# Two merged loads of a linear-attention and SwiGLU kernel as four loads of 128 pieces

## The chip, the core and the metric

The kernel runs on one core of one Trainium2 chip. TensorE (PE in the profile) multiplies matrices, with weight loads in a row of their own (PEld); VectorE (DVE), ScalarE (ACT) and GpSimd (POOL) do the elementwise work; SyncE (SP) issues most transfers. The metric is the device time of one launch in microseconds.

## The reference, cut to what matters

The input x is 2048 rows of 512 bf16 values. The output is x plus a linear-attention block plus a gated feed-forward block, both of the layer-normalised rows xn.

```python
xn = _layernorm(x, axis=-1)
return x + _A_ref(xn, A_wqkv, A_wo) + _B_ref(xn, B_w_gate, B_w_up, B_w_down)
# A: q, k, v = xn @ wqkv in 32 heads of 16;  phi(t) = where(t > 0, t + 1, exp(t)) + 1e-6
#    kv = phi(k)^T v;  z = sum of phi(k);  o = (phi(q) kv) / (phi(q) z + 1e-6);  o @ wo
# B: (silu(xn @ w_gate) * (xn @ w_up)) @ w_down
```

## The kernel before

The 2048 rows are cut into 16 tiles of 128 rows, one row per partition. For each tile the program takes mean and variance (bn_stats, line 300, and bn_aggr, line 303), forms xn, transposes it, projects it to K and Q with 4 matmuls each (contraction of 512 in 4 blocks of 128), turns K and Q into their positive features, and adds the outer product of xn and the K features into four PSUM banks (gtacc, line 668). After the 16 tiles come 56 steps of the feed-forward block (line 870), between which the attention is divided by its denominator (lines 1015 to 1057) and output tiles are made and stored (lines 1059 to 1094).

The program is a list of instructions written out by hand, one list per engine, each run in order. A helper (line 43) adds the waits that reads and writes of named buffers need; every transfer has a semaphore of its own. So the place of a call in the source is its place in its engine's queue, and an engine that waits holds up all that stands behind it.

Tiles 0 to 3 go another way than the rest. K and Q are projected from the centred tile, and the division by the standard deviation is put into ScalarE's reading of the projection. Tiles 0 and 1 are centred on TensorE: traw (line 440) transposes the raw tile with an identity, and tcorr (line 452) adds minus the mean with a matmul of ones by a diagonal. For tile 0 that diagonal (line 401) comes from a sum of the row's two halves on VectorE (line 391), for tile 1 from ScalarE (line 308). Tile 2 is centred on VectorE (line 381) and transposed on TensorE (line 488). Tile 3 is centred on VectorE (line 470) and transposed by a transfer (line 479).

The order of the projections of tiles 0 to 3 is by hand as well (lines 720 to 817). Q's third block (c = 2) is used for tile 0, then for tile 1; then the fourth (c = 3) for tile 0, its PSUM bank is read by ScalarE (line 618), and the fourth for tile 1 (lines 752 to 756). Each such matmul (line 543) waits for its own block's name, and one load that brings two blocks sets both names at once. Then follow both projections of tile 2 and K features of tile 0 on GpSimd (line 625); gtacc of tile 0; tile 3 (line 530); gtacc of tiles 1 and 2. VectorE's list in the same part is: statistics of tiles 1, 2; centring of 2; statistics of 3; line 583 for tile 0; centring of 3; statistics of 4, 5, 6; then xn (line 317) and the K features (line 632) of the first tiles.

The loads stand ahead of all that (lines 253 to 263), on SyncE's queue, in the order x 0, K's blocks 0 and 1, K's block 2, x 2, Q's block 0, Q's block 1, x 3, Q's blocks 2 and 3, x 4 and 5, x 6 and 7; x 1 and K's block 3 go by ScalarE's queue. The remaining x tiles go in pairs behind tile 3's transpose (lines 737, 738, 773, 810).

How rows lie in tiles is set by NLONE (line 200). A tile below NLONE holds 128 successive rows, so that each partition gets one piece of 1 KB per tile. The rows from NLONE on are dealt out so that a partition holds successive rows in successive tiles: a load of two such tiles is 128 pieces of 2 KB. The same function (line 202) maps the output's rows, so input and output agree. A weight block is 128 rows of 1 KB; a load of two blocks is 256 pieces.

Of the kernel before, what the change touches and what calls it, by code (L numbers as in the profile page):

```python
# [109 lines left out]
def bass_parallel_sum__linear_attn_block__swiglu_ffn__prompt_kernel(  # L110
# [13 lines left out]
    pe, act, dve, pool, sp = nc.tensor, nc.scalar, nc.vector, nc.gpsimd, nc.sync  # L124
    bf, f32 = dt.bfloat16, dt.float32

    with contextlib.ExitStack() as es:
# [69 lines left out]

        NLONE = 4  # L200

        def rows(v, t0, n):
            if t0 < NLONE:
                return v[t0 * P:(t0 + n) * P, :].rearrange("(t p) d -> p t d", p=P)
            return v[NLONE * P:, :].rearrange("(p t) d -> p t d", t=NT - NLONE)[:, t0 - NLONE:t0 - NLONE + n, :]

        def xload(eng, h, t0, n, after=()):
            K.dma(
                eng, lambda: h.dma_start(x_sb[:, t0:t0 + n, :], rows(xin, t0, n)),  # L209
                r=list(after), w=[("x", t0 + i) for i in range(n)],  # L210
            )

        def wqkv_load(eng, h, name, i, c0, n, after=()):
            K.dma(
                eng,
                lambda: h.dma_start(  # L216
                    wqkv_sb[:, c0:c0 + n, i * D:(i + 1) * D],
                    A_wqkv[c0 * P:(c0 + n) * P, i * D:(i + 1) * D].rearrange("(c p) f -> p c f", p=P),
                ),
                r=list(after), w=[(name, c) for c in range(c0, c0 + n)],  # L220
            )
# [36 lines left out]
        wqkv_load("sp", sp, "wq", 0, 0, 1)  # L258
        wqkv_load("sp", sp, "wq", 0, 1, 1)
        xload("sp", sp, 3, 1)  # L260
        wqkv_load("sp", sp, "wq", 0, 2, 2)
        xload("sp", sp, 4, 2)
        xload("sp", sp, 6, 2)

        cw = nc.const_aps.tensor(1.0, (P, P), bf)
# [907 lines left out]
```

## Time and profile before

| what | value |
|---|---|
| median of 3 runs | 210.54 us (210.31 to 211.08) |
| profiled execution | 210.56 us |
| its span | 209.3 us |
| TensorE busy | 205.0 us (98%) |
| VectorE, ScalarE, GpSimd busy | 119.7, 71.8, 72.2 us |
| TensorE's granted clock | 1.00 |
| read from HBM | 9.70 MB |

The span runs from the first to the last recorded instruction or transfer; the device time holds a little more around it. A line of the timeline gives start and duration in us, engine, line of the source, operation, what is written from what, shapes, and a count; in square brackets stands how long the engine had been idle before and what ended that. [...] A row of a transfer group gives the size in KB and the time from its issue to its landing.

### The profile page before, as it was taken

The numbers are of one execution on the slowest core, as the hardware profiler recorded it, in microseconds if no ns is written. First come the engines' busy times: TensorE is split into PE (matmuls) and PEld (weight loads), VectorE is DVE, ScalarE is ACT, GpSimd is POOL, SyncE is SP. The second block draws the span as 40 slices with busy tenths as digits, with TensorE's granted clock in tenths as the row PEclk, the third lists the DMA queues.
The fourth block names the chain that finished last, engine by engine and source line by source line (L and its number), as shares of the span: only waits on it lengthen the run. The fifth ranks groups of instructions, "written<-read, shape, count | busy, mean of one in ns | idle before, by whom it ended". The sixth has DMA issues, their size and how long they took to land.

```text
span 209.3 us, 2809 instructions
## 1 busy us (share of the span) xinstructions
PE 205.0 (98%) x998; PEld 94.5 (45%) x1017; DVE 119.7 (57%) x245; ACT 71.8 (34%) x127; POOL 72.2 (34%) x91
## 2 busy tenths in 40 slices
PE   8999999999999999999999999999999999999996
PEld 4444444444444444444444444444444444444444
DVE  4799988336365874637355746365556545374122
ACT  6877666966643331312112312213031213121000
POOL 2537987668032543223041422240424132221200
PEclk9999999999999999999999999999999999999999
DMA  6765645894696011010201110102011010110201
GB/s 197 219 184 79 127 100 102 258 364 153 206 356 49 11 39 25 28 25 25 52 0 50 28 28 22 50 0 53 5 45 25 25 28 28 49 27 27 53 25 50
DMA packets 30127, 16.84 MB, mean 80 GB/s; under 512 B 20896, under 2 KB 29344, under 8 KB 30112
## 3 DMA queue, kind: packets, MB, share of 16 engines
q1 hardware_dynamic: 29824, 16.39, 30.0%
q10 hardware_dynamic: 288, 0.26, 0.4%
q8 instruction: 8, 0.13, 0.2%
q14 instruction: 7, 0.06, 0.1%
HBM read 9.70 MB, written 2.10 MB: 56 GB/s over the span
## 4 chain that ended last, share of the span: by engine, by line
PE 91%; DVE 3%; DMA 2%; SPq 1%; issue 1%; POOL 1%; DVEq 0%
PE psum L870 44%; PE psum L1075 23%; PE psum L516 9%; PE psum L1064 7%; PE psum L668 6%; DMA wqkv_sb<-in_A_wqkv_dram 2%; PE psum L530 2%; SPq L216 1%; DVE pkq L592 1%; SPq L209 1%; POOL prod L1019 1%; PE psum L543 0%; DVE xn_sb L317 0%; DVE den L1027 0%; DVE pkq L891 0%
## 5 line engine op out<-in xcount | busy, mean ns | idle before, releaser
L885 ACT ACTIVATE sg<-psum 128x512 bf16<-128x512 f32 x56 | 33.4, 599 | 106.0 <-PE psum L870 103.6
L870 PE MATMUL psum<-xnT,wg_sb 128*128 128x512 bf16 x222 | 57.2, 379 | 0.2 <-issue 0.2
L870 PE MATMUL psum<-xnT,wu_sb 128*128 128x512 bf16 x216 | 55.8, 379 | 0.4
L1019 POOL TENSOR_TENSOR prod<-pkq,zb 128x512 f32<-128x512 bf16 x16 | 18.6, 1163 | 55.9 <-DVE pkq L592 55.9
L870 PEld LDWEIGHTS psum<-xnT,wu_sb 128*128 128x128 bf16 x224 | 21.9, 98 | 26.4
L870 PEld LDWEIGHTS psum<-xnT,wg_sb 128*128 128x128 bf16 x224 | 21.7, 98 | 26.2 <-issue 0.2
L1088 DVE TENSOR_TENSOR out_sb<-psum,x_sb 128x512 bf16<-128x512 f32 (+2 forms) x17 | 11.2, 661 | 36.2 <-PE psum L1075 36.2
L1043 POOL TENSOR_TENSOR pqn<-pkq,rden 128x512 bf16<-128x512 bf16 x16 | 16.9, 1058 | 36.6 <-DVE rden L1037 36.6
L891 DVE TENSOR_TENSOR pkq<-psum,sg 128x512 bf16<-128x512 f32 x28 | 19.2, 686 | 17.1 <-PE psum L870 14.6
L891 DVE TENSOR_TENSOR xn_sb<-psum,sg 128x512 bf16<-128x512 f32 x28 | 18.8, 672 | 13.8 <-PE psum L870 13.3
L1075 PE MATMUL psum<-wd_sb,xn_sb 128*128 128x512 bf16 (+2 forms) x126 | 25.7, 355 | 0.0
L1075 PE MATMUL psum<-wd_sb,pkq 128*128 128x512 bf16 x108 | 25.1, 379 | 0.2
L516 PE MATMUL psum<-wqkv_sb,xnT 128*128 128x512 bf16 x95 | 22.5, 379 | 0.1
L660 POOL TENSOR_TENSOR zacc<-zacc,pkq 128x512 f32<-128x512 f32 x15 | 17.4, 1157 | 5.0 <-DVE ek L583 4.6
L1075 PEld LDWEIGHTS psum<-wd_sb,xn_sb 128*128 128x128 bf16 x126 | 11.8, 98 | 12.5
L1075 PEld LDWEIGHTS psum<-wd_sb,pkq 128*128 128x128 bf16 x112 | 11.0, 98 | 13.2
L1064 PE MATMUL psum<-m_sb,eq 128*128 128x512 bf16 (+2 forms) x67 | 16.4, 366 | 0.1
L668 PE MATMUL psum<-pkq,xn_sb 128*128 128x512 bf16 x61 | 15.6, 379 | 0.2
L516 PEld LDWEIGHTS psum<-wqkv_sb,xnT 128*128 128x128 bf16 x96 | 9.4, 98 | 11.3
L1027 DVE TENSOR_REDUCE den<-prod 128x32 f32<-128x512 f32 x16 | 10.9, 684 | 5.9 <-POOL prod L1019 5.9
L300 DVE BATCH_NORM_STATS2 stats<-x_sb 128x6 f32<-128x512 bf16 x16 | 10.9, 680 | 1.1 <-DMA x_sb<-in_A_x_dram 1.1
L592 DVE SCALAR_TENSOR_TENSOR pkq<-pkq,eq 128x512 bf16<-128x512 bf16 x16 | 11.1, 692 | 0.6
(78 smaller groups left out, 139.7 us busy)
## 6 DMA issues: line engine op xcount, KB each, us to landing
out_dram<-out_sb SPq DMA_DIRECT2D x15, 128.0 KB, 1.7
wg_sb<-in_B_w_gate_dram SPq DMA_DIRECT2D x2, 896.0 KB, 7.5
wu_sb<-in_B_w_up_dram SPq DMA_DIRECT2D x2, 896.0 KB, 5.9
wd_sb<-in_B_w_down_dram SPq DMA_DIRECT2D x1, 1792.0 KB, 11.1
x_sb<-in_A_x_dram SPq DMA_DIRECT2D x6, 256.0 KB, 3.2
wqkv_sb<-in_A_wqkv_dram SPq DMA_DIRECT2D x2, 256.0 KB, 3.6
wqkv_sb<-in_A_wqkv_dram SPq DMA_DIRECT2D x1, 512.0 KB, 7.7
wo_sb<-in_A_wo_dram SPq DMA_DIRECT2D x1, 512.0 KB, 8.7
```

Of the source, the lines that this page charges most:

```text
L516: (lambda c=c: pe.matmul(banks[b], xnT[:, c, t * P:(t + 1) * P], wqkv_sb[:, c, lo:lo + D], start=(c == 0), stop=(c == NDC - 1),))
L592: lambda: dve.scalar_tensor_tensor(out=dst, in0=src, scalar=0.0, in1=e, op0=ALU.max, op1=ALU.add,),
L660: lambda: pool.tensor_tensor(out=zacc[:, :], in0=zacc[:, :], in1=pk, op=ALU.add),
L668: (lambda c=c: pe.matmul(banks[4 + c], xn_sb[:, t, c * P:(c + 1) * P], pkq[:, t, 0, :], start=(t == 0), stop=(t == NT - 1),))
L870: (lambda c=c: pe.matmul(banks[b], w_sb[:, c, fc * P:(fc + 1) * P], xnT[:, c, C * 512:(C + 1) * 512], start=(c == 0), stop=(c == NDC - 1),))
L885: lambda: act.activation(sg[:, j % NSG, :], banks[gb], ACT.Silu),
L891: lambda: dve.tensor_tensor(out=hT(C, fc), in0=banks[ub], in1=sg[:, j % NSG, :], op=ALU.mult,),
L1019: lambda: pool.tensor_tensor(out=p, in0=pkq[:, t, 1, :], in1=zb[:, :], op=ALU.mult),
L1043: lambda: pool.tensor_tensor(out=pqn[:, t % NPN, :].rearrange("p (i g h e) -> p g i h e", i=NB, g=NG, e=DH), in0=pkq[:, t, 1, :].rearrange ...
L1064: (lambda g=g: pe.matmul(dst, pqnT(t)[:, g, :], m_sb[:, g, lo:hi], start=(g == 0), stop=False,))
L1075: (lambda fc=fc: pe.matmul(dst, hT(C, fc)[:, jj * P:(jj + 1) * P], wd_sb[:, fc, lo:hi], start=False, stop=(fc == NFC - 1),))
L1088: lambda: dve.tensor_tensor(out=o, in0=src, in1=x_sb[:, t, lo:hi], op=ALU.add),
```

## The change

The boundary NLONE goes from 4 to 6, so tiles 4 and 5 hold 128 successive rows each, and the ten tiles behind them are dealt out over partitions in tens rather than twelves, in input and output alike. The merged load of Q's blocks 2 and 3 becomes two loads, and the merged load of x 4 and 5 becomes two loads, in the same place of SyncE's queue. Tile 0's mean from two half sums, named with the change, is in the kernel before already (lines 388 to 406) and not in the diff.

```diff
-        NLONE = 4
+        NLONE = 6
 
         def rows(v, t0, n):
             if t0 < NLONE:
@@
         xload("sp", sp, 3, 1)
-        wqkv_load("sp", sp, "wq", 0, 2, 2)
-        xload("sp", sp, 4, 2)
+        wqkv_load("sp", sp, "wq", 0, 2, 1)
+        wqkv_load("sp", sp, "wq", 0, 3, 1)
+        xload("sp", sp, 4, 1)
+        xload("sp", sp, 5, 1)
         xload("sp", sp, 6, 2)
```

## The prediction

> **What bounds the kernel now.** I read the page first, then the busy time of each engine by stretch, then the chain of waits and the merged timeline of the first 20 us.
>
> ```profile
> span 209.3 us, 2809 instructions
> PE 205.0 (98%) x998; PEld 94.5 (45%) x1017; DVE 119.7 (57%) x245; ACT 71.8 (34%) x127; POOL 72.2 (34%) x91
> ```
> ```profile
> 0.00:8.36 8.36, 7.03 (x35) 3.29 (x36) 4.47 (x15) 6.12 (x14) 2.89 (x13) 1.00 0.78 233
> 8.36:20.00 11.64, 11.59 (x53) 5.30 (x55) 10.92 (x31) 8.47 (x16) 6.05 (x10) 1.00 0.50 132
> 20.00:47.20 27.20, 27.04 (x124) 12.35 (x126) 18.77 (x42) 19.49 (x36) 20.63 (x30) 1.00 0.72 187
> 47.20:207.50 160.30, 159.39 (x788) 73.56 (x801) 85.31 (x158) 37.72 (x63) 42.64 (x40) 1.00 0.20 51
> ```
>
> In the second fence the first two numbers are the stretch and its length, the third PE's busy time. TensorE is idle 1.33 us before 8.36 and nearly never after it (0.05, 0.16 and 0.91 us in the other stretches, at a granted clock of 1.00). So TensorE sets the end, and a gain can only come from the idle time ahead of 8.36; it reaches the end if nothing behind 8.36 is late for the earlier TensorE. The span is 209.3 us, the profiled execution took 210.56 us, so 1.26 us lie around the span; the median of the runs is 210.54, so a sum against the profiled execution stands for the median too.
>
> The last wait on a transfer is the one that the change touches:
>
> ```profile
> 4.12 4.19 DMA wqkv_sb<-in_A_wqkv_dram
> 8.36 1.04 PE psum L543 x4
> ```
> ```profile
> 3.65 0.43 SPq L209 DMA_DIRECT2D x_sb<-in_A_x_dram  x1
> 4.12 0.44 SPq L216 DMA_DIRECT2D wqkv_sb<-in_A_wqkv_dram  x1
> 4.61 0.94 SPq L209 DMA_DIRECT2D x_sb<-in_A_x_dram  x2
> 8.36 1.04 PE L543 MATMUL psum<-wqkv_sb,xcT 128*128 128x512 bf16 x4 [0.50 <-DMA wqkv_sb<-in_A_wqkv_dram]
> 9.15 0.69 DVE L300 BATCH_NORM_STATS2 stats<-x_sb 128x6 f32<-128x512 bf16 x1 [0.38 <-DMA x_sb<-in_A_x_dram]
> ```
>
> The merged load of Q's blocks 2 and 3 is issued at 4.12 and lands at 8.31; TensorE sat idle 0.50 us for it. The merged load of x 4, 5 is issued behind it, and VectorE sat idle 0.38 us until bn_stats of tile 4 at 9.15. These two waits are all that the change can take away.
>
> **The change, part by part.** SyncE issues one load per 0.47 us whatever its size (3.65 to 4.12). Now: wq block 2 at 4.12, block 3 at 4.59, x 4 at 5.06, x 5 at 5.53, x 6, 7 at 6.00 instead of 5.08. Two issues are added, 0.94 us of SyncE's queue. The next instruction there is a transpose that waits for VectorE until 8.79:
>
> ```profile
> 8.79 1.29 SPq L479 DMA_TRANSPOSE xcT<-xc_sb  x1
> 10.13 1.04 SPq L209 DMA_DIRECT2D x_sb<-in_A_x_dram  x2
> ```
>
> SyncE is free at about 6.5, 2.3 us ahead of it: no cost. Without this cover it would be the 0.94 us itself. No instruction of another engine is added or moved. Tile 0's half sums (line 391) and their diagonal (line 401) stand in the code of before and not in the diff, so this half of the title costs and brings nothing.
>
> When do the four loads land? Issue to landing of the single loads, then of the merged ones (median in the last column), in order of issue: wq 0, wq 1, x 3; then wq 2 with 3, x 4 with 5, x 6 with 7.
>
> ```profile
> wqkv_sb<-in_A_wqkv_dram SPq DMA_DIRECT2D x1, 128.0 KB, 3.7
> wqkv_sb<-in_A_wqkv_dram SPq DMA_DIRECT2D x1, 128.0 KB, 3.6
> x_sb<-in_A_x_dram SPq DMA_DIRECT2D x1, 128.0 KB, 3.5
> ...
> wqkv_sb<-in_A_wqkv_dram SPq DMA_DIRECT2D x1, 256.0 KB, 4.2
> ...
> x_sb<-in_A_x_dram SPq DMA_DIRECT2D x1, 256.0 KB, 4.5
> ...
> x_sb<-in_A_x_dram SPq DMA_DIRECT2D x1, 256.0 KB, 4.7
> ```
>
> A 128 KB load per 0.47 us keeps the delay level (3.7, 3.6, 3.5), so the backlog does not grow; 256 KB per issue makes it grow. The price of a single load at this place has no row. Lower bound 3.5 us from its issue, as x 3 just ahead; upper bound the merged loads' 4.2 to 4.7. I take 3.5, the nearest row of the same size: wq 2 at 7.6, wq 3 at 8.1, x 4 at 8.6, x 5 at 9.0, x 6, 7 at 9.5 to 10.7 (3.5 to 4.7 from 6.00).
>
> [...]
>
> Pieces: the page of the transfers shows the merged x loads as 2 KB pieces, the rest as 1 KB.
>
> ```profile
> DMA packets 448, 0.67 MB, mean 223 GB/s; under 512 B 49, under 2 KB 193, under 8 KB 448
> ```
>
> That is the window 6.5 to 9.5: 255 packets lie between 2 and 8 KB, which are the 128 pieces each of x 4, 5 and x 6, 7 but one. After it x 4, 5 are 256 pieces of 1 KB; the bytes are the same.
>
> Three places then decide how much of 0.50 us survives.
>
> **First, TensorE.** Transposes end at 7.48 + 0.39 = 7.87.
>
> ```profile
> 7.48 0.39 PE L488 MATMUL psum<-ident,xc_sb 128*128 128x128 bf16 x4
> ```
>
> Two of the four matmuls need only block 2, and they are first in TensorE's order (lines 752 to 756). One matmul is 0.216 us (1.73 us for 8 in the chain, the row at 9.40 below). Two of them run from 7.87 to 8.30 while block 3 lands by 8.1. Gain 0.50, or 0.49 if block 3 lands at 8.31 as the merged one. Upper bound of all that follows: 0.50.
>
> ```profile
> 9.40 1.73 PE psum L530 x8
> ```
>
> **Second, tile 3's transposed copy.** It does not move: VectorE centres tile 3 ahead of any of these loads, the transpose is issued at 8.79 and lands 2.5 us later, at 11.29.
>
> ```profile
> xcT<-xc_sb SPq DMA_TRANSPOSE x1, 2.5
> ```
> ```profile
> 10.95 0.70 ACT L606 ACTIVATE kpos<-psum,rstd 128x512 f32<-128x512 f32 x1
> 11.70 1.52 PEld L530 LDWEIGHTS psum<-wqkv_sb,xcT 128*128 128x128 bf16 x8 [0.20 <-ACT kpos L606]
> 11.82 1.89 PE L530 MATMUL psum<-wqkv_sb,xcT 128*128 128x512 bf16 x8
> ```
>
> Its first weight load ran at 11.70, 0.05 us behind ScalarE's 11.65, and its matmul at 11.82. ScalarE's row of activations starts from the third of the four matmuls (9.22 below) and moves with TensorE, so ScalarE would allow 11.70 - 0.50. The transpose allows 11.29 + 0.05 = 11.34 and a matmul at 11.46. Gain here: 0.36 us.
>
> ```profile
> 9.22 0.69 ACT L618 ACTIVATE pkq<-psum,rstd 128x512 bf16<-128x512 f32 x1 [0.77 <-PE psum L543]
> ```
>
> **Third, VectorE.** From 9.15 to 14.20 it works without a gap, and TensorE's second block of K-feature products waits for its end:
>
> ```profile
> 13.51 0.69 DVE L632 TENSOR_TENSOR pkq<-kpos,ek 128x512 bf16<-128x512 f32 x1
> 13.55 1.89 PE L668 MATMUL psum<-pkq,xn_sb 128*128 128x512 bf16 x8
> 14.25 0.70 PEld L668 LDWEIGHTS psum<-pkq,xn_sb 128*128 128x128 bf16 x4 [0.17 <-DVE pkq L632]
> ```
>
> The fifth of those eight matmuls is due at 13.55 + 4 x 0.216 = 14.41; its weight load at 14.25 with the same 0.12 us behind it as above (11.70 to 11.82) allows 14.37. Slack 0.04. So TensorE gains here only what VectorE gains, plus 0.04. VectorE is free at 8.77:
>
> ```profile
> 8.42 0.35 DVE L470 TENSOR_SCALAR xc_sb<-x_sb,mv 128x512 bf16<-128x512 bf16 x1
> ```
>
> If x 4 has landed by then (I have 8.6), the run starts 0.38 earlier; x 5 is needed at 9.6 (have 9.0), x 6 at 10.4 (have 9.5 to 10.7, so up to 0.3 could be lost at its far end). GpSimd allows it: its sum of K features ends at 8.66 + 1.16 = 9.82, and tile 4's rstd then comes 0.33 earlier than it did behind the row at 10.15, while its reader is VectorE at 11.74.
>
> ```profile
> 8.66 1.16 POOL L625 TENSOR_TENSOR pkq<-kpos,ek 128x512 bf16<-128x512 f32 x1 [0.45 <-DVE ek L583]
> 10.15 0.23 POOL L345 TENSOR_SCALAR vpe<-mv 128x2 f32<-128x2 f32 x1 [0.34 <-DVE mv L303]
> 11.74 0.73 DVE L317 TENSOR_SCALAR xn_sb<-x_sb,mv,rstd 128x512 bf16<-128x512 bf16 x2
> ```
>
> Gain here: 0.38 + 0.04 = 0.42.
>
> The sum is the least of the three, 0.50, 0.36 and 0.42: **0.36 us**. Behind it the transposes of tile 4 onward follow VectorE, which is earlier too, and the first FFN weights have room:
>
> ```profile
> 36.81 0.58 SPq L231 DMA_DIRECT2D wg_sb<-in_B_w_gate_dram  x1
> wg_sb<-in_B_w_gate_dram SPq DMA_DIRECT2D x1, 896.0 KB, 5.0
> ```
>
> They land at 41.8, TensorE wants them at 47.2. The boundary of the plain rows goes from tile 4 to tile 6, so x 8 to 15 and the stores keep their pieces and only change the step between rows. No row prices that. The first of those loads is issued at 10.13, at 4.7 us it would land by 14.83, and VectorE reads tile 8 only eight instructions behind its run to 14.20: nothing. The last two stores, of 96 and 32 KB:
>
> ```profile
> out_dram<-out_sb SPq DMA_DIRECT2D x1, 96.0 KB, 1.6
> out_dram<-out_sb SPq DMA_DIRECT2D x1, 32.0 KB, 1.4
> ```
>
> They keep their pieces too; between the two rows lie 0.2 us, which I take as the bound either way, and nothing as the value.
>
> 210.56 - 0.36 = 210.20 us.
>
> **The rivals.** *The split loads land at the merged pace.* The merged wq pair took 1.16 us behind x 3, 0.58 per 128 KB. Then wq 2 at 7.73, wq 3 at 8.31, x 4 at 8.89. TensorE still gains 0.49, but VectorE starts tile 4 at 8.93: gain 0.22 + 0.04 = 0.26, 210.30 us. For it: that pace stands right at this place. Against it: 0.36 per load just ahead.
>
> *The x half is hidden or absent.* x 4 lands no earlier than 9.1 (the same bytes through the same engines). Then VectorE is where it was, and only its slack of 0.04 remains: 210.52 us, whatever Q gains.
>
> [...] Landing is issue plus what the merged loads showed: wq 3 at 4.59 + 4.2 = 8.79, x 4 at 5.06 + 4.5 = 9.56. The place is bn_stats of tile 4: it starts 0.44 later, TensorE loses 0.44 - 0.04 = 0.40 at the fifth product: 210.96 us, slower. It decides once x 4 lands more than 4.1 us behind its issue. For it: the delays only rise from 4.2 to 4.7. Against it: these are the 256 KB loads, and the level 3.7 to 3.5 of the 128 KB ones.
>
> **How the numbers follow.** Forecast 0.50; merged pace 0.18; hidden 0.12; own delay 0.12; something outside these 0.08. A measurement of this kernel tells about 0.5% (1.05 us) from no change, and all four named cases lie within it; 0.50 us is the most that the idle time in reach allows. Of what is outside and of the scatter I give 0.04 to faster by over 0.5%, 0.08 to slower, 0.88 to within. The range: the low end is the full 0.50 (210.06) less the 0.23 that the fastest run of before lay under its median, 209.8; the high end is the third rival, 211.0.
>
> **What would show it.** Right: TensorE's wait on the wq load gone, its four matmuls from 7.9; bn_stats of tile 4 at 8.8; tile 3's first matmul at about 11.46 behind the transpose, and the span 0.36 shorter. Wrong: x 4 landing after 8.8 (rivals one and two), after 9.15 (three), a wait for x 6 at 10.4, or TensorE idle behind 15 us, where I have none.

## The result, and the profile after

| what | before | after |
|---|---|---|
| median of 22 runs each, taken side by side | 210.62 us (210.31 to 211.08) | 210.28 us (209.81 to 210.95) |
| profiled execution | 210.56 us | 210.39 us |
| its span | 209.3 us | 209.2 us |

The ratio is 0.9982, 95% interval 0.9974 to 0.9991: 0.38 us less, between 0.19 and 0.55 (the two medians lie 0.34 us apart). The forecast was 0.36 us less.

The landings first, in the view of the transfers of the changed kernel; the last column is the time from issue to landing, in order of issue: wq 2, wq 3, x 4, x 5, then x 6 with 7.

```profile
wqkv_sb<-in_A_wqkv_dram SPq DMA_DIRECT2D x1, 128.0 KB, 3.5
...
wqkv_sb<-in_A_wqkv_dram SPq DMA_DIRECT2D x1, 128.0 KB, 3.3
x_sb<-in_A_x_dram SPq DMA_DIRECT2D x1, 128.0 KB, 3.7
...
x_sb<-in_A_x_dram SPq DMA_DIRECT2D x1, 128.0 KB, 3.5
x_sb<-in_A_x_dram SPq DMA_DIRECT2D x1, 256.0 KB, 3.6
```

The merged ones took 4.2, 4.5 and 4.7. Here the delay stays level. The timeline of the changed kernel, at the places that were shown of before:

```profile
4.12 0.91 SPq L216 DMA_DIRECT2D wqkv_sb<-in_A_wqkv_dram  x2
4.69 1.06 PE L545 MATMUL psum<-wqkv_sb,xcT 128*128 128x512 bf16 x2
5.07 1.38 SPq L209 DMA_DIRECT2D x_sb<-in_A_x_dram  x3
5.75 2.39 PE L545 MATMUL psum<-wqkv_sb,xcT 128*128 128x512 bf16 x10
7.98 0.39 PE L490 MATMUL psum<-ident,xc_sb 128*128 128x128 bf16 x4
8.21 1.03 PE L545 MATMUL psum<-wqkv_sb,xcT 128*128 128x512 bf16 x4
8.40 0.26 DVE L585 TENSOR_SCALAR ek<-ek 128x512 bf16<-128x512 bf16 x1
8.84 0.69 DVE L302 BATCH_NORM_STATS2 stats<-x_sb 128x6 f32<-128x512 bf16 x1
8.95 1.29 SPq L481 DMA_TRANSPOSE xcT<-xc_sb  x1
11.66 1.89 PE L532 MATMUL psum<-wqkv_sb,xcT 128*128 128x512 bf16 x8
13.39 1.89 PE L670 MATMUL psum<-pkq,xn_sb 128*128 128x512 bf16 x8
```

Lines of the source are two further down than before. The four wq matmuls at 8.21 and bn_stats of tile 4 at 8.84 have no idle time in brackets: both waits that the change aimed at are gone. Tile 3's first matmul is at 11.66 (before 11.82), and everything behind it is 0.16 us earlier, as is the end. So this pair of executions shows 0.17 us of the 0.38; the rest lies between executions, which scatter by more than this (209.81 to 210.95 us for the changed kernel).

But 8.21 is not 7.87, and what held TensorE there is not a load. The busy times by stretch of the changed kernel:

```profile
0.00:8.36 8.36, 7.52 (x36) 3.74 (x37) 4.34 (x14) 5.61 (x13) 2.87 (x13) 1.00 0.74 223
```

TensorE is idle 0.84 us before 8.36, all of it ahead of its first matmul; before it was 1.33. Compare the same two K matmuls in the timeline of the kernel before:

```profile
4.69 0.64 PE L543 MATMUL psum<-wqkv_sb,xcT 128*128 128x512 bf16 x2
```

0.64 us for two there, 1.06 us in the changed kernel. In this execution TensorE still ran at its opening half pace at 4.69 (0.85 us for two matmuls of 512 columns in the chain of waits, 0.43 each; later 1.73 us for eight, 0.216 each), and reached the wq matmuls 0.34 us later than the forecast had it. The kernel before has a wait at this place that swallows such a delay; the changed kernel has none.

Nor is 7.87 the moment at which TensorE could have gone on in the kernel before: a group's length in the timeline is more than its share of TensorE's time (eight matmuls of 512 columns read 1.89 us there and 1.73 in the chain of waits). Here the wq matmuls start 0.23 us behind the start of the transposes (7.98 and 8.21), whose row reads 0.39 us, and the same step from 7.48 gives 7.71. Counted from start to start, the wait before was about 0.65 us, not 0.50, and TensorE came 0.50 us later in this execution.

### The profile page after: what moved, and what is told of

The parts are those of the page before. It is cut to its first block, busy times and chain, and to the rows that moved or that the text cites. A ratio compares the mean times of both kernels' runs of the same rounds, so it can differ in the third digit from the quotient of the medians.

```text
span 209.2 us, 2811 instructions
## 1 busy us (share of the span) xinstructions
PE 205.4 (98%) x998; PEld 94.8 (45%) x1017; DVE 119.6 (57%) x245; ACT 71.8 (34%) x127; POOL 72.1 (34%) x91
## 4 chain that ended last, share of the span: by engine, by line
PE 97%; DVE 1%; issue 1%
PE psum L872 46%; PE psum L1077 23%; PE psum L518 9%; PE psum L1066 7%; PE psum L670 6%; PE psum L545 2%; PE psum L532 2%; PE psum L274 1%; PE psum L454 0%; PE psum L442 0%; DVE xn_sb L319 0%; DVE pkq L594 0%; PE psum L979 0%; DVE stats L302 0%; PE psum L1002 0%
```

## The experiments

All ratios are to the kernel before, run on the same chip beside them. Theory A is the prediction's: TensorE's wait, tile 3's transpose and VectorE's run from tile 4's statistics each limit the gain, and the least counts. The rivals that were set against it: B, TensorE's wait on the wq load alone decides; C, the kind of pieces decides; D, what limits the changed kernel is TensorE's slow pace at the start, which the kernel before hides; E, that pace does not matter.

**Q's blocks alone.** The kernel before (NLONE 4, x 4, 5 merged) with this edit:

```diff
-        wqkv_load("sp", sp, "wq", 0, 2, 2)
+        wqkv_load("sp", sp, "wq", 0, 2, 1)
+        wqkv_load("sp", sp, "wq", 0, 3, 1)
```

> Only Q's blocks 2 and 3 are split; x 4, 5 stay one load of 128 pieces of 2 KB and the row boundary stays at tile 4. Theory A (least of three places): block 2 lands at 7.6, block 3 at 7.9 to 8.3, TensorE's wait goes, but x 4, 5 land at about 9.1 as before, bn_stats of tile 4 starts at 9.1, and the fifth K-feature product stays at about 14.4: the gain is VectorE's slack of 0.04 us, ratio 0.999 to 1.000. Theory B (TensorE's wait on the wq load alone decides): the whole gain of the change, about 0.35 us, ratio 0.998.

Measured: 210.70 us (12 runs), ratio 0.9986, interval 0.9970 to 1.0002. That does not separate A from B: the interval holds both, and the ratio is that of the changed kernel's second measurement below (0.9986). So the times do not show that splitting x 4, 5 adds anything to splitting Q's blocks. The timeline shows where this execution stood:

```profile
7.77 0.59 PE L544 MATMUL psum<-wqkv_sb,xcT 128*128 128x512 bf16 x2
8.84 0.61 PE L544 MATMUL psum<-wqkv_sb,xcT 128*128 128x512 bf16 x2 [0.47 <-DMA wqkv_sb<-in_A_wqkv_dram]
9.52 0.69 DVE L301 BATCH_NORM_STATS2 stats<-x_sb 128x6 f32<-128x512 bf16 x1 [1.07 <-DMA x_sb<-in_A_x_dram]
```

The first two wq matmuls no longer wait; block 3, split but with a merged x load behind it, lands late (4.2 us from its issue, expected 3.3 to 3.7), and TensorE waits 0.47 us between the two blocks. x 4, 5 lands at 9.5 and VectorE idles 1.07 us. Splitting the Q blocks moved the wait; it did not remove it in this execution.

**x 4 and x 5 alone.** The changed kernel (row boundary at tile 6) with Q's blocks 2 and 3 merged:

```diff
-        wqkv_load("sp", sp, "wq", 0, 2, 1)
-        wqkv_load("sp", sp, "wq", 0, 3, 1)
+        wqkv_load("sp", sp, "wq", 0, 2, 2)
```

> Only x 4 and x 5 are split (row boundary at tile 6); Q's blocks 2 and 3 stay one load. Theory A: the merged block pair lands at 8.3, TensorE waits 0.5 us as before and nothing behind it can win that back: ratio 1.000, bn_stats of tile 4 at 8.8 instead of 9.15. Theory B': the x loads alone bring the gain by way of VectorE: ratio 0.998. If the pair lands earlier because the x pieces behind it are different ones, TensorE's matmuls start before 8.3 and the gain is that difference.

Measured: 210.91 us, ratio 0.9999, interval 0.9989 to 1.0009. No gain, as A said; but bn_stats of tile 4 stood at 9.24 and not at 8.8, since the merged pair landed at 8.9 and x 4 behind it at 9.2. In the timeline:

```profile
8.93 1.04 PE L544 MATMUL psum<-wqkv_sb,xcT 128*128 128x512 bf16 x4 [0.23 <-DMA wqkv_sb<-in_A_wqkv_dram]
9.24 0.69 DVE L301 BATCH_NORM_STATS2 stats<-x_sb 128x6 f32<-128x512 bf16 x1 [0.46 <-DMA x_sb<-in_A_x_dram]
```

So the result is A's, and one part of its reason (x 4 early) is not.

**The row boundary alone.** The kernel before (both loads merged) with NLONE 6, so that x 4, 5 is one load of 256 pieces of 1 KB:

```diff
-        NLONE = 4
+        NLONE = 6
```

> Both loads stay merged, the row boundary goes to tile 6, so that x 4, 5 is one load of 256 pieces of 1 KB. Theory A: the pair of blocks lands at 8.3 and x 4, 5 at 9.1 as before, ratio 1.000. Theory C (it is the kind of pieces or the addresses, not the number of loads): the landings come as early as in the changed kernel, 7.9 for the pair and below 9.0 for x 4, 5, and the ratio is 0.998.

Measured: 210.99 us, ratio 1.0001, interval 0.9982 to 1.0019; the loads took 4.1 and 4.4 us to land. Pieces and addresses bring nothing that could be seen. The pair landed at 8.2 and not at C's 7.9, and x 4, 5 at 9.0, and the interval ends just above C's 0.998. So theory C falls, though by one execution and a wide interval. In this execution TensorE came at 8.62, by a slow opening (1.06 us for the two K matmuls at 4.99), and did not wait for the pair at all.

**VectorE's limit, made worse.** The changed kernel with x 4 behind x 6, 7:

```diff
-        xload("sp", sp, 4, 1)
         xload("sp", sp, 5, 1)
         xload("sp", sp, 6, 2)
+        xload("sp", sp, 4, 1)
```

> The changed kernel with x 4 issued behind x 6, 7 instead of ahead of x 5, so that x 4 lands last, at about 9.7. Theory A: VectorE's run starts at 9.7 instead of 9.15 in the kernel before, the fifth K-feature product comes 0.5 us late, and the time is 0.4 to 0.5 us over the kernel before, ratio 1.002, although TensorE's wait at 8.3 is gone. Theory B: only the wq loads matter, ratio 0.998 as with the change.

Measured: 211.12 us (12 runs), ratio 1.0015, interval 1.0007 to 1.0024. Slower, against B; A's 1.002 lies in the interval. The timeline:

```profile
7.58 1.24 PE L545 MATMUL psum<-wqkv_sb,xcT 128*128 128x512 bf16 x4
9.77 0.69 DVE L302 BATCH_NORM_STATS2 stats<-x_sb 128x6 f32<-128x512 bf16 x1 [1.17 <-DMA x_sb<-in_A_x_dram]
11.26 1.89 PE L532 MATMUL psum<-wqkv_sb,xcT 128*128 128x512 bf16 x8
13.74 1.52 PE L670 MATMUL psum<-pkq,xn_sb 128*128 128x512 bf16 x5 [0.60 <-DVE pkq L634]
14.87 0.11 PEld L670 LDWEIGHTS psum<-pkq,xn_sb 128*128 128x128 bf16 x2 [0.58 <-DVE pkq L634]
```

TensorE was 0.56 us earlier than before at tile 3 (11.26 against 11.82) and gave all of it back, and more, to VectorE: the second block of K-feature products got its weights at 14.87, before at 14.25. VectorE's limit is real once x 4 comes this late.

**The transpose's limit, made worse.** The changed kernel with tile 3's centring behind tile 4's statistics:

```diff
-        xc_full(3)
         bns(4)
+        xc_full(3)
```

> The changed kernel with the centring of tile 3 moved behind the statistics of tile 4 in VectorE's list, so that tile 3's transpose is issued about 1 us later, at 9.8, and lands at about 12.3. Theory A (three places, the second is tile 3's transposed copy): TensorE waits for it, the first matmul of tile 3 is at about 12.4 instead of 11.7, and the time is 0.4 to 0.7 us over the kernel before, ratio 1.002 to 1.003. Theory B (only the wait on the wq load counts, the transpose has room): ratio 0.998 as with the change.

Measured: 211.20 us (11 runs), ratio 1.0018, interval 1.0008 to 1.0028, just under A's 1.002 to 1.003, which the interval reaches into, and against B. The timeline:

```profile
7.96 1.03 PE L545 MATMUL psum<-wqkv_sb,xcT 128*128 128x512 bf16 x4
9.95 1.29 SPq L481 DMA_TRANSPOSE xcT<-xc_sb  x1
12.58 1.89 PE L532 MATMUL psum<-wqkv_sb,xcT 128*128 128x512 bf16 x8 [1.00 <-DMA xcT<-xc_sb]
```

The transpose, which took 2.5 us from issue to landing in the views of both kernels, is issued at 9.95 here, and TensorE waits 1.00 us for it. 1.00 us later in issue (9.95 against 8.95) cost 0.92 us at tile 3 (12.58 against 11.66): in the changed kernel the transpose had less than 0.1 us of room. The median moved less, 0.38 us over the kernel before, 0.76 us over the changed one if that keeps its 0.9982.

**TensorE's opening pace, both kernels.** One instead of five opening dummy matmuls, in the kernel before and in the changed one:

```diff
-        fill(5, 512)
+        fill(1, 512)
```

> The kernel before with 1 instead of 5 of the opening dummy matmuls of 512 columns, so that TensorE is idle from about 1.5 to 3.0 and its matmuls go to the fast pace later. Theory D (what the changed kernel still lacks is TensorE's slow pace at the start, which the wait on the wq load hides in the kernel before): some of the delay is hidden by the wait, the rest shows, 0.3 to 1.2 us over the kernel before, ratio 1.001 to 1.006. Theory E (the pace at the start does not matter, the loads do): ratio 1.000.

> The changed kernel with the same 1 instead of 5 opening matmuls. Theory D: TensorE reaches the wq matmuls after the loads in both kernels, so the gain of the change is gone: the ratio to the kernel before equals that of the other short-fill kernel within 0.001. Theory E: the change keeps its gain, this kernel lies 0.35 us (0.0017) under the other short-fill kernel.

Measured: before with the short opening 211.12 us, ratio 1.0018 (1.0005 to 1.0031); changed with it 210.87 us, ratio 1.0014 (0.9997 to 1.0031). The ratios differ by 0.0004, within D's 0.001, but each interval is 0.003 wide, so E's 0.0017 is not excluded by the times. The timelines, kernel before first:

```profile
5.86 2.68 PE L543 MATMUL psum<-wqkv_sb,xcT 128*128 128x512 bf16 x10
8.59 1.03 PE L543 MATMUL psum<-wqkv_sb,xcT 128*128 128x512 bf16 x4
```
```profile
5.84 3.59 PE L545 MATMUL psum<-wqkv_sb,xcT 128*128 128x512 bf16 x10
9.49 1.03 PE L545 MATMUL psum<-wqkv_sb,xcT 128*128 128x512 bf16 x4
```

TensorE was idle for 1.56 and 1.64 us here until its transposes at 2.98 and 3.07, and the two K matmuls at 4.68 and 4.77 took 1.06 us in both. In neither do the wq matmuls wait for a load any more: the ten matmuls ahead of them took 2.68 and 3.59 us instead of 2.36 and 2.39 with the long opening, and in this pair the changed kernel was the later one. Times of the changed kernel with the short opening ran from 210.39 to 211.94 us, those of the kernel before on that chip from 210.21 to 211.43. So D holds in these two executions; how large it is on average stays open.

The traces show an opening at half the later pace (0.43 and 0.216 us per matmul in the chain of the changed kernel), and that it ends at different moments (0.64 and 1.06 us for the same two matmuls at 4.69); the granted clock in the profile stood at 1.00 throughout and did not show it. What sets that moment is not shown: in the twelve executions with the long opening the ten matmuls took 2.32 to 2.81 us, and the 2.68 of the kernel before with the short one lies among them.

**A clip on GpSimd**, to move both of VectorE's limits out:

```diff
-        clip_k(0)
+        clip(ek[:, 0, :], ("ek", 0), "pool")
```

> The changed kernel with the clip of tile 0's K exponentials on GpSimd instead of VectorE, where it stands ahead of the centring of tile 3. Theory A: VectorE's list is 0.25 us shorter ahead of tile 3's transpose and tile 4's statistics, both limits of VectorE move out by up to 0.25 us and the gain goes from 0.36 towards TensorE's 0.50: ratio 0.9975 to 0.998. Theory D: the pace of TensorE at the start sets what is left, so nothing is won over the change: ratio 0.998.

Measured: 211.07 us, ratio 1.0012, interval 1.0000 to 1.0023. Both theories missed. The timeline:

```profile
7.69 1.96 POOL L586 TENSOR_SCALAR ek<-ek 128x512 bf16<-128x512 bf16 x1 [1.75 <-ACT ek L603]
10.82 0.69 ACT L603 ACTIVATE ek<-psum,rstd 128x512 bf16<-128x512 f32 x1 [0.59 <-POOL rstd L356]
11.97 1.04 PE L671 MATMUL psum<-pkq,xn_sb 128*128 128x512 bf16 x3 [0.52 <-POOL pkq L628]
```

The clip takes 1.96 us there and 0.26 on VectorE (8.40 in the changed kernel's timeline), and it stands ahead of the reciprocal roots for which ScalarE, and through it TensorE, wait. I had priced only VectorE's side. The profiled execution was the slowest of the twelve (211.69 us), and in its timeline the wq matmuls came late too, at 8.70, so not all of its delay is the clip's.

**The changed kernel and the kernel before once more**, for second executions:

> The changed kernel once more, for its time on another chip and for a second profiled execution. Theory A: ratio 0.998; where TensorE's pace goes up early (the first two K matmuls of tile 0 at 0.22 us apart), its wq matmuls start at 7.6 to 7.9 and tile 3's first matmul waits for its transpose at 11.3 to 11.5. Theory D: where the pace goes up late (0.43 us apart), the wq matmuls start behind 8.0 without a wait for a load, and the execution keeps less than 0.36 us of gain.

> The kernel before once more, for a second profiled execution: the pair of Q blocks lands at 8.1 to 8.9 and x 4, 5 at 9.0 to 9.5, both later than in any execution of the kernels with four single loads (7.9 to 8.1, 8.5 to 8.8).

Measured: the changed kernel 210.59 us (11 runs), ratio 0.9986, interval 0.9976 to 0.9996; the kernel before in its one run 210.85 us. The timeline of the changed kernel:

```profile
4.67 0.59 PE L545 MATMUL psum<-wqkv_sb,xcT 128*128 128x512 bf16 x2
5.76 2.32 PE L545 MATMUL psum<-wqkv_sb,xcT 128*128 128x512 bf16 x10 [0.39 <-DMA wqkv_sb<-in_A_wqkv_dram]
8.13 1.03 PE L545 MATMUL psum<-wqkv_sb,xcT 128*128 128x512 bf16 x4
11.59 1.89 PE L532 MATMUL psum<-wqkv_sb,xcT 128*128 128x512 bf16 x8
```

and of the kernel before:

```profile
8.65 1.04 PE L543 MATMUL psum<-wqkv_sb,xcT 128*128 128x512 bf16 x4 [0.35 <-DMA wqkv_sb<-in_A_wqkv_dram]
9.26 0.69 DVE L300 BATCH_NORM_STATS2 stats<-x_sb 128x6 f32<-128x512 bf16 x1 [1.00 <-DMA x_sb<-in_A_x_dram]
12.11 1.89 PE L530 MATMUL psum<-wqkv_sb,xcT 128*128 128x512 bf16 x8
```

The pace was up early this time (0.59), yet TensorE came at 8.13 again: an earlier wait, for a block of K, took 0.39 us. So neither theory had this execution: A expected 7.6 to 7.9, D a slow pace as the cause of anything later. And the kernel before was later than in its first profile: its merged pair landed 4.5 us from its issue instead of 4.2, within what was expected, and tile 3's first matmul came at 12.11 instead of 11.82. TensorE's opening was slow there as well (1.06 us for the two K matmuls at 4.63): its transposes, at 7.92 in that timeline, were 0.44 us later than in the first profile, and the wait took the delay up. That is what D says the kernel before does.

**The clip behind the centring**, both still on VectorE:

```diff
-        clip_k(0)
         xc_full(3)
+        clip_k(0)
         bns(4)
```

> The changed kernel with the clip of tile 0's K exponentials behind the centring of tile 3 on VectorE, both still ahead of tile 4's statistics: tile 3's transpose is issued 0.17 us earlier, nothing else moves. Theory A: the second limit goes from 0.36 to about 0.5 and the third (0.42) decides, 0.06 us at most over the change: ratio 0.9975 to 0.998. Theory D: ratio 0.998, nothing won, since TensorE's pace at the start decides.

Measured: 210.15 us, ratio 0.9968, interval 0.9955 to 0.9980, from 6 runs against 11 of the changed kernel beside it. It is the lowest of all, and its interval lies wholly below 1; against the changed kernel on that chip (0.9976 to 0.9996) the intervals still touch. A's range of 0.9975 to 0.998 lies in it, and D's 0.998 on its edge, so it does not decide between them. In the profiled execution, the slowest of the six at 210.55 us, the wq matmuls started at 8.36 behind another wait for a block of K, and the transpose was issued at 8.35, well ahead of its use:

```profile
5.07 0.96 PE L545 MATMUL psum<-wqkv_sb,xcT 128*128 128x512 bf16 x2 [0.27 <-DMA wqkv_sb<-in_A_wqkv_dram]
8.35 1.28 SPq L481 DMA_TRANSPOSE xcT<-xc_sb  x1
11.81 1.89 PE L532 MATMUL psum<-wqkv_sb,xcT 128*128 128x512 bf16 x8
```

It shows no gain of its own, so why the time is lower is not shown.

**x 4, 5 as one load of 1 KB pieces**, Q's blocks split:

```diff
-        xload("sp", sp, 4, 1)
-        xload("sp", sp, 5, 1)
+        xload("sp", sp, 4, 2)
```

> Q's blocks split, row boundary at tile 6, and x 4, 5 as one load of 256 pieces of 1 KB. Theory A: block 3 lands by 8.3, but x 4 lands with x 5 at 9.1, so VectorE's run starts at 9.1 and the gain is 0 to 0.1 us, ratio 0.9995 to 1.000. If the length of the pieces was what held block 3 up where x 4, 5 was one load of 2 KB pieces (4.2 us from issue to landing), it lands 3.5 us from its issue here; if it is the size of the load behind it, 4 us or more again.

Measured: 210.52 us (11 runs), ratio 0.9991, interval 0.9982 to 0.9999. The timeline:

```profile
7.94 1.04 PE L544 MATMUL psum<-wqkv_sb,xcT 128*128 128x512 bf16 x4
9.12 0.69 DVE L301 BATCH_NORM_STATS2 stats<-x_sb 128x6 f32<-128x512 bf16 x1 [0.81 <-DMA x_sb<-in_A_x_dram]
14.23 0.55 PEld L669 LDWEIGHTS psum<-pkq,xn_sb 128*128 128x128 bf16 x4 [0.56 <-DVE pkq L633]
```

This is VectorE's limit as the prediction drew it: the wq matmuls are 0.42 us earlier than before, x 4, 5 lands at 9.1 as before, and the second block of K-feature products gets its weights at 14.23, against 14.25 before. It took back 0.25 us and not all: tile 4's projections, which follow these products, start at 15.11 here and at 15.28 before, so 0.17 us of the 0.42 are left. Block 3 landed 3.6 us from its issue here, so the 4.2 of the first experiment may come from the 2 KB pieces behind it; one execution of each does not settle it.

## Why the prediction was right, point by point

*The landings* were sized right to 0.2 us. Forecast 7.6, 8.1, 8.6 and 9.0; from issue and delay, 7.6, 7.9, 8.8 and 9.0. In the seven profiled executions with four single loads (x 4 last in one of them) block 3 took 3.3 to 3.6 us; a merged Q pair took 3.9 to 4.8 us in five. But block 3 is issued 0.47 us later, so by landing the ranges are 7.9 to 8.2 and 8.0 to 8.9, and they touch; what the split brings in all seven is the first block, at 7.3 to 7.7. Of the rivals, the third (each load its own delay, 210.96 us) and the second (x half hidden, 210.52 us) lie outside the interval. The first, the merged pace with 0.26 us, lies inside it: the time does not rule it out. Its landings of Q's blocks do (block 3 at 8.31, measured 7.9), while x 4 at 8.77 is nearer to its 8.89 than to the 8.6 of the forecast. Nor did the split loads take the merged ones' 4.2 and 4.5 us, as the third rival had it: they took 3.5, 3.3, 3.7 and 3.5. The 0.36 us per load that spoke against the first rival are x 3 behind wq 1 in the kernel before (7.15 and 6.78).

*First place, TensorE.* This term was mis-sized, from both sides. The wait went, as forecast, and counted from start to start it was about 0.65 us and not 0.50. But TensorE arrived at 8.21 and 8.13 in two executions, once because its pace went up later, once because of a wait for a block of K. I had read its arrival off one execution as if nothing ahead of it varied, and had taken idle time for all that could change: two K matmuls that take 1.06 us instead of 0.64 are a loss without any idle time. On the other side the kernel before also varies: 8.36 and 8.65. Between the means of the two pairs, 8.505 and 8.17, lie 0.34 us, near the 0.36 forecast and the 0.38 measured. Two profiles of each kernel are few, so this agreement is an argument and no proof.

*Second place, the transpose.* Named as the one that decides, at 11.46. In the two executions of the changed kernel it did not decide: tile 3 came at 11.66 and 11.59 without a wait for it. It is close behind. Where TensorE did wait for it, tile 3 came 2.63 us behind its issue (9.95 and 12.58), so issues at 8.95 and 8.82 allowed 11.58 and 11.45, 0.08 and 0.14 us ahead of TensorE. In the execution with x 4 last, where TensorE came to the wq matmuls at 7.58, tile 3 came at 11.26, just 2.63 us behind the issue at 8.63: there the two met. And "it does not move" was wrong. In the executions that keep VectorE's order the transpose was issued anywhere from 8.29 to 8.98, mostly as x 2 landed earlier or later (3.2 to 4.0 us from its issue), so 11.46 too was the value of one execution.

*Third place, VectorE.* Right in kind: late x 4 turned a gain into a loss, and x 4, 5 in one load took back 0.25 us of the Q gain at the K-feature products. Its slack was mis-sized. In that last execution the fifth product can be placed from tile 4's projections at 15.11: four products of 0.216 us ahead of them give 14.25, only 0.02 us behind its weights at 14.23, where the prediction allowed 0.12. So the slack before was about 0.14 us and not 0.04 (an estimate). A gain of that size, a ratio of 0.9993, lies in the intervals of both kernels with the Q blocks split and x merged (0.9986 and 0.9991). How much splitting x adds to splitting Q's blocks is not shown by any time here.

*Nothing behind 15 us* took the gain back. The start of tile 4's projections tells it, in the kernel before and in the changed one:

```profile
15.28 1.03 PE L516 MATMUL psum<-wqkv_sb,xnT 128*128 128x512 bf16 x4
15.11 1.24 PE L518 MATMUL psum<-wqkv_sb,xnT 128*128 128x512 bf16 x5
```

The 0.17 us between them is the difference of the two times. In the eleven profiled executions whose views show this start, of nine kernels, the time is this start plus 195.27 to 195.28 us. So whatever differs in them, between kernels and between executions of one kernel, has happened by then. Taken there, the two executions of the kernel before (15.28, 15.57) and the two of the changed one (15.11, 15.04) lie 0.35 us apart in the mean. The unmoved costs, two more issues on SyncE (0.91 us for both loads of wq and 1.38 for the three of x, all ahead of the transpose at 8.95) and the row boundary, are covered as forecast: boundary alone 1.0001.

So the sum came out right, its place did not: the least of the three was TensorE's own arrival, not the transpose. That the number agrees so closely is in part luck. The forecast was a difference within one execution, the measured 0.38 us is a difference between executions whose arrivals scatter by as much, and two of its three terms were mis-sized. What was understood is that the wait on Q's blocks would go and that the next limits lie close behind it.

## What to carry to other kernels

In the full queue of early loads here, what mattered was when the first needed bytes land: with Q's blocks split the first load of 128 KB landed at 7.3 to 7.9 us in nine executions and one of 256 KB at 8.0 to 8.9 in five, the second of 128 KB mostly sooner too (7.9 to 8.8), and the consumer could start on the first half. Removing a wait is worth only as much as the next limit allows, so find the next ones (here the engine's own arrival, a transpose and another engine's run within 0.2 us of each other). That moving them together pays is not shown here: the one attempt to move two of them, the clip on GpSimd, was slower. And a wait in a profile may be hiding scatter ahead of it: read the arrival time from more than one execution before sizing what its removal brings.

## What had not been expected of the hardware

The opening half pace of TensorE ended at different moments in executions of the same program: two K matmuls at 4.7 us took 1.06 us in one execution and 0.59 in the other, while the granted clock in the profile read 1.00. And a clip of 128x512 bf16 values that takes VectorE 0.26 us took GpSimd 1.96.
